# Products of zeros on TensorE from the first microsecond, and the first stages by head pairs, in a fused attention and FFN kernel

## The chip, the cores and the metric

One core of one Trainium2 chip. Times are device microseconds of one execution; a quoted time is the median of the runs named. The span is the time from a kernel's first to its last instruction in the trace. In the views of the profile PE stands for TensorE's products, PEld for its weight loads, DVE for VectorE, ACT for ScalarE and POOL for GpSimd. PSUM is the memory of the kernel's `ps_` tiles, which products are written to; a bank is the place of one such tile. A load *lands* when its data are all there.

## The reference, cut to what matters

```python
# q, k, v: (8, 8, 1024, 64)   batch, heads, tokens, head size;   E, F: (64, 1024)
k_proj = einsum('ks,bhsd->bhkd', E, k)
v_proj = einsum('ks,bhsd->bhkd', F, v)
scores = q @ k_proj^T / 8
attn = exp(scores) / sum(exp(scores))
x = (attn @ v_proj), heads side by side: (8192, 512)
h = maximum(x @ w_in, 0)          # w_in: (512, 2048)
out = (h * h) @ w_out             # w_out: (2048, 512), out float32
```

## The kernel before

Eight batches. While the FFN of one batch runs, pieces of the attention of the next stand between its groups of matmuls. Only batch 0 has no FFN to hide behind, so it has a routine of its own, `first_stages`, that works on half of the tokens first so that the FFN can start early. All matmuls take bf16. The order of instructions on every engine is the order in which they are written, and the trace has them in it: K's first half landed at 8.72 us, and its products started at 9.11, behind two fillers written ahead of them that started at 8.14.

The loads of batch 0 are issued from the GpSimd queue in the order of need, one behind the other:

```python
for s in (slice(0, 4), slice(4, 8)):
    load_heads(K_first, k, s)            # K in two halves (heads 0-3, 4-7)
...
load_q_half(0, slice(0, H))              # Q, first half of the tokens
for s in (slice(0, 4), slice(4, 6), slice(6, 8)):
    load_heads(V_first, v, s)            # V in three pieces
nc.scalar.preload_act_table_set("natural_log_exp_and_others")
ones = const_pool.tile([P, 32], BF16, name="ones")
nc.vector.memset(ones[:], 1.0)
...                                      # then w_in in pieces, w_out, Q's second half
```

The first stages. `filler` multiplies data that are there anyway, into a PSUM bank that nobody reads, to keep TensorE active:

```python
def first_stages(self):
    def filler(n):
        ps = ffn_psum("ps_fill")
        for _ in range(n):
            nc.tensor.matmul(ps[:], lhsT=ET[:, 0:2, :], rhs=ET[:], start=True, stop=True)
    filler(2)
    self.project_k(0)                    # 8 products 128x256, waits for K's first half
    filler(1)
    self.transpose_k(0)
    self.project_k(1)                    # waits for K's second half
    filler(2)
    self.transpose_k(1)
    filler(1)
    for g in range(2):
        self.half_transpose_q(0, g, ffn_psum)      # waits for Q
    for g in range(2):
        self.half_scores(0, g)
        self.half_exponentials(g)
    heads = [slice(0, 4), slice(4, 6), slice(6, 8)]
    self.project_v(heads[0])
    self.copy_v(heads[0])
    self.half_sums(0, apart=True)
    self.half_sums(1)
    self.half_reciprocals(0)
    self.half_reciprocals(1)
    self.half_values(0)
    for s in heads[1:]:
        self.project_v(s)
        self.copy_v(s)
    self.half_values(1)
    for g in range(2):
        for e in range(2):
            self.half_normalize(0, g, e)
```

Then the FFN. Its opening takes four groups at once, column block by column block (16 products), which is why "the fifth group" is a landmark below.

The softmax here doesn't subtract the row's maximum and nothing guards it: scores larger than these inputs give would overflow.

Of the kernel before, what the change touches and what calls it, by code (L numbers as in the profile page):

```python
# [8 lines left out]
P = 128  # L9
F32 = mybir.dt.float32  # L10
BF16 = mybir.dt.bfloat16
# [9 lines left out]
def kernel(  # L21
# [11 lines left out]
    nc = tc.nc  # L33
# [20 lines left out]
    const_pool = ctx.enter_context(tc.tile_pool(name="const", bufs=1))  # L54
# [15 lines left out]
    def att_psum(shape, dtype):  # L70
        return aps.tile(shape, dtype, tag="att", name="ps_att")

    def ffn_psum(name, shape=(P, 512), dtype=F32):
        return fps.tile(list(shape), dtype, tag="ffn", name=name)
# [4 lines left out]
    def load(name, src, b):  # L79
        t = qkv_pool.tile([P, H, NI * D], BF16, name=name)  # L80
        nc.gpsimd.dma_start(t[:], rows(src, b))  # L81
        return t
# [18 lines left out]
    ident = const_pool.tile([P, P], BF16, name="ident")  # L101
# [3 lines left out]
        load_heads(V_first, v, s)  # L105
    nc.scalar.preload_act_table_set("natural_log_exp_and_others")
    ones = const_pool.tile([P, 32], BF16, name="ones")
    nc.vector.memset(ones[:], 1.0)


# [22 lines left out]

    LO, HI = slice(0, 64), slice(64, 128)
    ET, FT = (const_pool.tile([P, NI, KP], BF16, name=n) for n in ("ET", "FT"))

    def E_and_F():
        for t, src, copy in ((ET, e_f32[0], nc.vector.tensor_copy), (FT, e_f32[1], nc.scalar.copy)):
            e_bf = soft_pool.tile([KP, S], BF16, tag="expT", name="e_bf")
            copy(e_bf[:], src[:])  # L140
            ps = ffn_psum("ps_E", (P, NI, KP), BF16)
            view = e_bf[:].rearrange("k (p i) -> k i p", i=NI)
            for i in range(NI):
                nc.tensor.transpose(ps[:, i, :], view[:, i, :], ident[0:KP, 0:KP])
            copy(t[:], ps[:])
# [7 lines left out]
    def combine_weights(q4, name):  # L153
        js = slice(4 * q4, 4 * q4 + 4)
        o, a, b = {"T1": (T1, W12, W11), "T2": (T2, W22, T1), "T3": (T3, W22, W12), "T4": (T4, W21, T2)}[name]
        nc.vector.tensor_tensor(out=o[:, js], in0=a[:, js], in1=b[:, js], op=ALU.subtract)
# [4 lines left out]
    class Attention:  # L161
# [127 lines left out]
                self.vp[:, s].rearrange("k h e d -> k e h d"),  # L289
                self.ps["vp", s.start][:].rearrange("k (h d e) -> k e h d", d=D // 2, e=2))  # L290

        def half_transpose_q(self, c, g, psum):
            ps = psum("ps_q", (P, 4, 2, P), BF16)
            for h in range(4):
                for n in range(2):
                    nc.tensor.transpose(
                        ps[:, h, n], self.Q[:, 4 * g + h, (2 * c + n) * P:(2 * c + n + 1) * P], ident[:])
            qt = self.qT[:].rearrange("p (h n) t -> p h n t", n=NT)
            nc.vector.tensor_copy(qt[:, 4 * g:4 * g + 4, 2 * c:2 * c + 2], ps[:])

        def half_scores(self, c, g):
            ps = self.ps["s", g] = att_psum([P, 2, 2, TH], F32)
# [52 lines left out]
            )  # L355

        def first_stages(self):
            def filler(n):
                ps = ffn_psum("ps_fill")
                for _ in range(n):  # L360
                    nc.tensor.matmul(ps[:], lhsT=ET[:, 0:2, :], rhs=ET[:], start=True, stop=True)

            filler(2)
            self.project_k(0)
            filler(1)
            self.transpose_k(0)
            self.project_k(1)
            filler(2)
            self.transpose_k(1)
            filler(1)  # L370
            for g in range(2):
                self.half_transpose_q(0, g, ffn_psum)
            for g in range(2):
                self.half_scores(0, g)
                self.half_exponentials(g)
            heads = [slice(0, 4), slice(4, 6), slice(6, 8)]
            self.project_v(heads[0])
            self.copy_v(heads[0])
            self.half_sums(0, apart=True)
            self.half_sums(1)  # L380
            self.half_reciprocals(0)
            self.half_reciprocals(1)
            self.half_values(0)
            for s in heads[1:]:
                self.project_v(s)
                self.copy_v(s)
            self.half_values(1)
            for g in range(2):
                for e in range(2):
                    self.half_normalize(0, g, e)  # L390

        def second_half(self, stage, g):
            if stage == 0:
                self.half_transpose_q(1, g, lambda name, shape, dtype: att_psum(shape, dtype))
            elif stage == 1:
                self.half_scores(1, g)
                self.half_exponentials(g)
            elif stage == 2:
                self.half_sums(g)
                self.half_values(g)  # L400
                self.half_reciprocals(g)
            else:
                for e in range(2):
                    self.half_normalize(1, g, e)
# [27 lines left out]
        53: "values 1 0, values 1 1", 54: "normalize 1 0", 55: "normalize 1 1",  # L432
    }
    SECOND_HALF = {
        7: "second_half 0 0", 9: "second_half 1 0", 10: "second_half 0 1",
        11: "second_half 2 0", 12: "second_half 1 1", 13: "second_half 3 0",
        15: "second_half 2 1", 16: "second_half 3 1",
    }
# [12 lines left out]
    def calls(table, n):  # L451
        for c in filter(None, table.get(n, "").split(", ")):
            name, *args = c.split()
            yield name, [int(a) for a in args]
# [232 lines left out]
    with tc.manual_schedule(engines=ORDERED):  # L687
        def load_batch(b):

            if b < B:  # L690
                order = [("K_sb", k), ("V_sb", v), ("Q_sb", q)] if b == 1 else [("Q_sb", q), ("K_sb", k), ("V_sb", v)]
                t = {n: load(n, src, b) for n, src in order}
                return Attention(b, t["Q_sb"], t["K_sb"], t["V_sb"])

        E_and_F()
        cur = Attention(0, Q_first, K_first, V_first)
        cur.first_stages()
        nxt = ahead = None
        for b in range(B):
            for n, g in enumerate(ffn_groups(b, cur.xT)):  # L700
                if b == 0:
                    for name, args in calls(SECOND_HALF, n):
                        getattr(cur, name)(*args)
                    for name, args in calls(WEIGHTS, n):
                        combine_weights(args[0], name)
                    if n == 31:
                        nxt = load_batch(1)
                if nxt:
                    for name, args in calls((BATCH_1, BATCH_2, PIECES)[min(b, 2)], n):
                        getattr(nxt, name)(*args)  # L710
                    if n == (35, 14, 1)[min(b, 2)]:
                        ahead = load_batch(b + 2)
                    if b and n == 33 and ahead:
                        ahead.transpose_q()
                    if b and n == 53 and ahead:
                        ahead.project()
                g()
            if b == 0:
                nxt.normalize(1, 1)
            cur, nxt, ahead = nxt, ahead, None  # L720
# [30 lines left out]
```

## Time and profile before

| what | kernel before | where from |
|---|---|---|
| device time | 483.68 us (483.64 to 484.29) | median of 3 runs |
| span of the profiled execution | 482.4 us | profile page |
| device time less span | 1.76 us (1.71 to 1.83) | mean of 48 runs, made beside the experiments and as `k1` |
| TensorE products | 3630, busy 470.3 us | profile page |
| VectorE instructions | 382 | profile page |
| loads of batch 0: K's first half, Q's first half | landed at 8.72 and 14.24 us | issue plus time to landing |

TensorE is busy 97% of the span, so there are some 12 us to be had at the very most, and 8.4 of them lie before 21 us. How the stages are read is told in the prediction.

### The profile page before, as it was taken

Reading aid. Unit: us, or ns where it says so; the run is one execution under the profiler, and the core shown is the slowest. Engines: PE = TensorE matmul, PEld = TensorE weight load, DVE = VectorE, ACT = ScalarE, POOL = GpSimd, SP = SyncE. Lnnn points to the kernel's source line nnn. Section 1 sums busy time; section 2 is a strip of 40 time slices with the busy share of each in tenths; the row PEclk is TensorE's granted clock in tenths of the full one; section 3 lists DMA queues with packets and bytes.
Section 4 is the critical chain, followed back from the end, with each engine's and each line's share of the span. In section 5 each row is a group of like instructions: output and inputs, shape, how many; then the busy total and the mean of one; then the engine's idle time right before and its main releaser. Section 6 shows DMA issues by size and latency. Waiting matters only on the chain.

```text
span 482.4 us, 8423 instructions
## 1 busy us (share of the span) xinstructions
PE 470.3 (97%) x3630; PEld 292.6 (61%) x3630; DVE 314.1 (65%) x382; ACT 261.5 (54%) x413; POOL 34.7 (7%) x48
## 2 busy tenths in 40 slices
PE   4899999999999999999999999999999999999997
PEld 2544676475574746657475665747557474666656
DVE  1478955554958559493776848667494855948383
ACT  2387544758427564466635667176662756545351
POOL 6540020020020001000010000100000000000000
PEclk9999999999999999999999999999999999999999
DMA  9999989579989086941859147690702102020202
GB/s 155 203 204 207 168 181 200 137 120 229 180 128 229 12 175 88 180 94 50 153 86 227 22 115 131 91 200 1 165 11 75 25 1 88 1 88 0 88 1 87
DMA packets 72789, 55.46 MB, mean 115 GB/s; under 512 B 33968, under 2 KB 64944, under 8 KB 72752
## 3 DMA queue, kind: packets, MB, share of 16 engines
q0 software_dynamic: 30624, 29.36, 39.4%
q1 hardware_dynamic: 42128, 25.56, 21.1%
q8 instruction: 28, 0.46, 0.4%
q14 instruction: 9, 0.07, 0.0%
HBM read 59.24 MB, written 16.78 MB: 158 GB/s over the span
## 4 chain that ended last, share of the span: by engine, by line
PE 92%; DVE 3%; DMA 3%; ACT 1%; POOL 1%; issue 0%; POOLq 0%
PE ps_h L459 44%; PE ps_y L479 23%; PE ps_z L479 11%; PE ps_x L479 6%; DMA V_sb<-in_v_dram 3%; PE ps_kv L180 2%; PE ps_att L221 2%; PE ps_att L206 2%; DVE hsq L521 1%; DVE s L473 1%; PE ps_v L284 0%; DVE xT L246 0%; DVE xT L351 0%; PE ps_kv L181 0%; ACT h_relu L513 0%; POOL K_sb L93 0%
## 5 line engine op out<-in xcount | busy, mean ns | idle before, releaser
L459 PE MATMUL ps_h<-xT,w_in 128*128 128x512 bf16 x1024 | 224.8, 379 | 0.2 <-DVE xT L351 0.2
L521 DVE TENSOR_TENSOR hsq<-h_relu 128x1024 bf16<-128x1024 f32 x123 | 149.9, 1222 | 75.0 <-ACT h_relu L513 74.2
L513 ACT ACTIVATE h_relu<-ps_h 128x512 f32<-128x512 f32 x255 | 149.4, 597 | 63.4 <-PE ps_h L459 63.0
L459 PEld LDWEIGHTS <-w_in 128*128 128x128 bf16 x1024 | 99.7, 98 | 117.7 <-issue 1.9
L479 PEld LDWEIGHTS <-s 128*128 128x128 bf16 x1024 | 98.5, 98 | 19.8 <-issue 8.7
L479 PEld LDWEIGHTS <-hsq 128*128 128x128 bf16 x768 | 73.8, 98 | 17.3 <-issue 3.8
L479 PE MATMUL ps_y<-T,s 128*128 128x256 bf16 x512 | 62.4, 273 | 0.0
L246 DVE TENSOR_TENSOR xT<-ps_att,rs 128x1024 bf16<-128x1024 f32 x28 | 33.4, 1215 | 17.6 <-ACT rs L236 17.0
L473 DVE TENSOR_TENSOR s<-hsq 128x1024 bf16<-128x1024 bf16 x64 | 43.5, 683 | 0.0
L591 ACT COPY o_sb<-ps_y 128x512 f32<-128x512 f32 x15 | 8.8, 586 | 53.8 <-PE ps_y L479 53.7
L213 ACT ACTIVATE expT<-ps_att 128x1024 bf16<-128x1024 f32 x28 | 27.2, 1025 | 14.0 <-PE ps_att L206 14.0
L479 PE MATMUL ps_x<-w_out,hsq 128*128 128x256 bf16 x256 | 33.2, 273 | 0.0
L479 PE MATMUL ps_y<-w_out,hsq 128*128 128x256 bf16 x256 | 33.2, 273 | 0.0
L595 DVE TENSOR_TENSOR o_sb<-ps_z,p_b 128x512 f32<-128x512 f32 x16 | 11.0, 688 | 33.8 <-issue 19.9
L479 PE MATMUL ps_y<-T,hsq 128*128 128x256 bf16 x256 | 30.9, 272 | 0.0
L479 PE MATMUL ps_z<-T,s 128*128 128x256 bf16 x256 | 30.6, 273 | 0.0
L479 PE MATMUL ps_z<-w_out,s 128*128 128x256 bf16 x256 | 30.6, 273 | 0.0
L591 ACT COPY p_b<-ps_y 128x512 f32<-128x512 f32 (+1 forms) x17 | 9.4, 556 | 25.9 <-PE ps_y L479 25.8
L81 POOL DMA_DIRECT2D Q_sb<-in_q_dram x7 | 6.1, 876 | 227.7 <-DMA qT<-Q_sb 227.2
L473 DVE TENSOR_TENSOR s<-s,hsq 128x1024 bf16<-128x1024 bf16 x32 | 21.8, 684 | 0.3
L473 DVE TENSOR_TENSOR s<-hsq,s 128x1024 bf16<-128x1024 bf16 x32 | 21.7, 682 | 0.0
L591 ACT COPY p_a<-ps_y 128x512 f32<-128x512 f32 (+1 forms) x17 | 9.4, 561 | 21.8 <-PE ps_y L479 21.6
(75 smaller groups left out, 233.0 us busy)
## 6 DMA issues: line engine op xcount, KB each, us to landing
out_dram<-o_sb SPq DMA_DIRECT2D x30, 512.0 KB, 3.8
K_sb<-in_k_dram POOLq DMA_DIRECT2D x7, 1024.0 KB, 15.3
V_sb<-in_v_dram POOLq DMA_DIRECT2D x7, 1024.0 KB, 22.4
Q_sb<-in_q_dram POOLq DMA_DIRECT2D x7, 1024.0 KB, 9.4
w_out<-in_moe_w_out_dram POOLq DMA_DIRECT2D x4, 512.0 KB, 13.2
w_in<-in_moe_w_in_dram POOLq DMA_DIRECT2D x7, 256.0 KB, 10.0
K_sb<-in_k_dram POOLq DMA_DIRECT2D x2, 512.0 KB, 8.5
out_dram<-o_sb SPq DMA_DIRECT2D x3, 256.0 KB, 2.1
```

The source lines that it names most:

```text
L180: nc.tensor.matmul(ps[0:KP, :], lhsT=ET[:, i, :], rhs=kv[:, :, i, :], start=f, stop=l)
L206: nc.tensor.matmul(ps[o, bank, :], lhsT=self.kT[r, 2 * pr + j, :], start=True, stop=True, rhs=self.qT[r, NT * (2 * pr + j):NT * (2 * pr + ...
L213: nc.scalar.activation(e[:], self.ps["s", pr][:], AF.Exp, scale=SCALE)
L221: nc.tensor.matmul(ps[32 * j:32 * j + 32, a, :], lhsT=weights(o, 4 * g + j), rhs=self.exp[2 * g + j // 2][o, bank, :], start=True, stop=Tr ...
L246: nc.vector.tensor_tensor(out=self.xT[:, 2 * g + e].rearrange("p a n t -> p a (n t)"), in0=self.ps["v", g, e][:], in1=self.rs[g][:], op=AL ...
L459: nc.tensor.matmul(ps[:], lhsT=w_in_blk(cb, fb), rhs=xT[:, cb, :, 2 * ch:2 * ch + 2], start=(cb == 0), stop=(cb == NCB - 1),)
L473: nc.vector.tensor_tensor(out=s[o][:, js], in0=x, in1=y, op=op)
L479: nc.tensor.matmul(ps[tb] if len(ps) == 2 else ps[0][:, tb], lhsT=lhs[:, j, tb * P:(tb + 1) * P], rhs=rhs[:, j], start=first and n == 0 an ...
L513: nc.scalar.activation(r[:, n], ps[:], AF.Relu)
L521: multiply = lambda: nc.vector.tensor_tensor(out=o, in0=r[:], in1=r[:], op=ALU.mult)
L591: nc.scalar.copy(to[:, t], ps)
L595: nc.vector.tensor_tensor(out=to[:, t], in0=ps, in1=more[:, t], op=ALU.add)
```

## The change

Its intent: in the trace of the kernel before, the first eight K products (from 9.11 us) take 1.92 us and the second eight (from 12.00) 1.06, and the clock's first record of full speed is at 11.23. So let TensorE multiply zeros from the first microsecond until E and then K land; let the copies of Q go in head pairs over two engines; and put the sums and normalizations of the first stages in an order that lets the FFN start earlier, with group 1's values inside the FFN's opening.

```diff
+    zeros = const_pool.tile([P, 512], BF16, name="zeros")
+    nc.vector.memset(zeros[:], 0.0)
     nc.vector.memset(ones[:], 1.0)
...
+    def filler(n):
+        ps = ffn_psum("ps_fill")
+        for _ in range(n):
+            nc.tensor.matmul(ps[:], lhsT=zeros[:, 0:P], rhs=zeros[:], start=True, stop=True)
...
         def first_stages(self):
-            filler(2)
+            filler(3)
             self.project_k(0)
-            filler(1)
+            filler(3)
             self.transpose_k(0)
             self.project_k(1)
-            filler(2)
+            filler(3)
             self.transpose_k(1)
-            filler(1)
-            for g in range(2):
-                self.half_transpose_q(0, g, ffn_psum)
+            for n in range(4):
+                self.half_transpose_q(
+                    0, range(2 * n, 2 * n + 2), ffn_psum, nc.scalar.copy if n == 1 else nc.vector.tensor_copy)
...
+            self.half_sums(0, apart=True)
             self.project_v(heads[0])
             self.copy_v(heads[0])
-            self.half_sums(0, apart=True)
             self.half_sums(1)
             self.half_reciprocals(0)
             self.half_reciprocals(1)
             self.half_values(0)
+            self.half_normalize(0, 0, 0)
             for s in heads[1:]:
                 self.project_v(s)
                 self.copy_v(s)
+            self.half_normalize(0, 0, 1)
+
+        def last_of_first(self):
             self.half_values(1)
-            for g in range(2):
-                for e in range(2):
-                    self.half_normalize(0, g, e)
+            for e in range(2):
+                self.half_normalize(0, 1, e)
...
     SECOND_HALF = {
-        7: "second_half 0 0", ...
+        1: "last_of_first", 7: "second_half 0 0", ...
...
+        filler(10)
         E_and_F()
```

## The prediction

> **What bounds the kernel now.** I began with the page's busy row and chain. TensorE is busy 470.3 of 482.4 us and carries 92% of the chain that ended last; the one DMA in that chain is V of the first batch. So there are two questions: how much of the 12 us without TensorE work lies in the stages that the change touches, and whether what is won there reaches the end. The stretches (columns: busy us and count of each engine, granted clock, DMA share, GB/s) answer the first:
>
> ```profile
> 0.00:8.72 8.72, 1.93 (x18) 1.29 (x18) 1.20 (x3) 2.80 (x3) 6.91 (x14) 1.00 0.79 139
> 8.72:14.24 5.52, 4.97 (x30) 2.69 (x28) 1.65 (x6) 0.11 (x1) 1.40 (x2) 1.00 1.34 201
> 14.24:21.05 6.81, 5.76 (x129) 3.81 (x129) 3.14 (x8) 4.34 (x7) 3.54 (x5) 1.00 1.28 204
> 21.05:24.70 3.65, 3.61 (x16) 1.56 (x16) 2.17 (x4) 0.64 (x2) 2.21 (x4) 1.00 1.30 200
> 24.70:53.30 28.60, 28.51 (x201) 13.11 (x201) 24.10 (x30) 23.30 (x39) 4.86 (x6) 1.00 1.25 206
> ```
>
> TensorE idles 6.8 us before K's first half, 0.55 and 1.05 us in the next two stretches, and practically never after 21 us. But the last column is level at 200 to 206 GB/s from 8.7 to 53.3 us: one uninterrupted stream of loads, the slower of two racers. So I read each early load's landing (issue plus time to landing): K 8.7 and 11.6 us; Q's first half 14.2; V 16.8, 18.1 and 19.4; w_in's first pieces 20.0, 20.7, 22.05, 23.3 and 24.55; Q's second half 25.9 and 29.8; w_in 27.2, 28.5, 31.1.
>
> Then I looked for the last place where TensorE meets the stream. It is the projection of batch 1, in the 34th group of the first FFN (columns: start, us, engine, line, operation):
>
> ```profile
> 53.03 0.40 PE L180 MATMUL ps_kv<-K_sb,ET 128*64 128x512 bf16 x1
> 53.32 0.38 PE L181 MATMUL ps_kv<-V_sb,FT 128*64 128x512 bf16 x1
> 53.32 0.40 PE L180 MATMUL ps_kv<-K_sb,ET 128*64 128x512 bf16 x1
> 53.53 0.38 PE L181 MATMUL ps_kv<-V_sb,FT 128*64 128x512 bf16 x1
> ...
> 54.82 0.38 PE L181 MATMUL ps_kv<-V_sb,FT 128*64 128x512 bf16 x1
> ```
>
> and the same stage of batch 2, where the data had landed earlier:
>
> ```profile
> 92.79 0.40 PE L180 MATMUL ps_kv<-K_sb,ET 128*64 128x512 bf16 x1
> 92.79 0.40 PE L181 MATMUL ps_kv<-V_sb,FT 128*64 128x512 bf16 x1
> ...
> 93.03 0.38 PE L180 MATMUL ps_kv<-K_sb,ET 128*64 128x512 bf16 x1
> ```
>
> In batch 2 V's first product starts with K's, at 92.79, and the next pair 0.24 us later. In batch 1 K's starts at 53.03 and V's only at 53.32. V was issued at 30.31 and takes 23.0 us to land:
>
> ```profile
> V_sb<-in_v_dram POOLq DMA_DIRECT2D x1, 1024.0 KB, 23.0
> ```
>
> that is 53.3 us. So **TensorE already waits about 0.29 us there for a transfer that the change does not touch.** "Idle" does not show it, because a pipelined K product's modelled end covers the gap.
>
> [...] the first eight K products (128x256) take 1.92 us, or (1.92 - 0.42) / 7 = 0.214 us apiece; the second eight, from 12.00 on, take 1.06 us, or 0.11. [...] V's issue occupies POOL for 0.88 us of the 23.0 to landing. Hence landings, not POOL's busy time, decide here.
>
> **The change part by part.**
>
> (1) Zero products. 13 more 128x512 fillers (10 in front, and 3+3+3 in place of 2+1+2+1). Ten at half speed cost about 0.40 us apiece (the two at 8.14 start 0.40 apart), about 4 us, from about 1.2 to at most 5.6. E's transposes, ready at 4.98, slip by up to 0.6 us, but TensorE then waits for F's cast until 7.49 anyway. Three warm fillers behind F (0.22 each, from the spacing of the 128x512 FFN products) end near 8.8, K's first half having landed at 8.7. The first K products now run warm and save 0.10 x 8 = 0.8 us, and nobody pays for the later fillers, since the next K half lands at 11.6. The second K half can start at 11.65 in place of 12.00. All of this ends at one line: Q's first half lands at 14.24, and before the change its transposes already start at 14.29. **Warmth buys 0 us past that point.**
>
> (2) Q by head pairs. The copies that gate group 0's scores were one of 0.68 us after 8 transposes (15.69 scores). Now: four transposes end at 14.67, DVE copies the pair by 15.1; pair 1's transposes end at 14.9 and ACT (0.59 us for 128x512 bf16, as FT's copy) is done by 15.5; scores complete about 15.6. The first exponential starts near 15.9 in place of 16.15, the second near 16.85 in place of 17.07: -0.2 us.
>
> (3) Sums ahead of V's projection. TensorE waits for the first exponential (about 16.95) and only then projects V, which landed at 16.78: projection from 17.1, not 16.82, and its copy at 18.6, not 18.35. So the values of group 0 come about 0.25 us later, while the reciprocals come 0.3 us earlier (19.16 for 19.48).
>
> (4) Normalization of group 0 between V's copies, group 1's values after the first FFN column block. Values 0 end at about 19.05, first normalization 19.2 to 19.9, V's two remaining projections end at 19.6 and 20.3 (before: 19.4 and 20.1). The first FFN products need w_in (20.0, 20.7) and start about 20.35 in place of 21.05. Then group 1's values (0.41 plus changeovers) stand inside the opening, and its 16 products take 3.6 us: 20.35 + 3.6 + about 0.5 = 24.4. Group 4 needs the PSUM bank of group 0, whose ReLU follows the first product of the last column block: about 24.4 in place of 24.70. **Gain at this point: 0.3 us.**
>
> (5) The 28.6 us that follow are the same instructions. The landings leave room for 0.3: the tightest, w_in at 28.49, is used at 29.03. So batch 1's projection is reached near 52.75, and V still lands at 53.3. The wait grows from 0.29 to about 0.6 us.
>
> Sum: -0.3 at 24.4, +0.3 at 53.3, **0 after that**; the rest is the old program at TensorE's pace.
>
> **The rivals.** (a) The gain survives: if V of batch 1 landed earlier, 0.3 us, perhaps 0.5, would reach the end, 483.2. For it: TensorE is busy without break from 21 us. Against: V is behind everything in one queue, and each issue on POOL from 9 us to 29 us follows a landing, so nothing that TensorE does earlier starts a transfer earlier. (b) The new order costs more than I count: in (3) TensorE stands in front of a projection whose data are there, and V's slot or DVE's order may cost 0.3 to 0.5 us more. The start of FFN would be 0.2 later than before; but the 0.29 us of waiting at 53.3 would swallow this too: 483.7 to 483.9. (c) The zero fill on DVE or longer POOL issues delay the start of the stream by 0.1 to 0.2 us: 483.8. (d) Warm clock as the whole intent: 0.8 us faster K projection, plus warm fillers, would give 482.7 if K's path set the end. Against it stands Q's landing at 14.24.
>
> **Range and chances.** The centre is the old 483.68 less a little for (a): 483.6. The old kernel's own three runs span 0.65 us, so the range is mostly that and the rivals: 483.0 to 484.2. 2% is 9.7 us; all of TensorE's idle time before 21 us is 8.4, so faster by that is out, and nothing in the change adds 9.7: 0.005, 0.99, 0.005.
>
> **What would show it.** Right: fillers from near 1.2 us; first K products about 0.11 us apart; Q's transposes still at about 14.3; first exponential about 15.9; first FFN product about 20.4; fifth group about 24.4; K's first product of batch 1 near 52.75 and V's first at 53.3 still, the gap between them doubled. Wrong: V of batch 1 landing clearly earlier or later than 53.3 (then the end moves with it); the first FFN product after 21; a new TensorE wait after 55 us.

(Two passages that no trace of this case shows are cut where marked. No term of the sum is among them: -0.3 us at the fifth group and +0.3 at the wait for V leave 0, and the centre is 483.6. That ten zero products in front are enough for the first K products to take 0.11 us apiece and not 0.214, as (1) has it, was my estimate.)

## More of the kernel before

In the 34th group stands the projection of batch 1's K and V, with the products of the two taking turns:

```python
BATCH_1 = {
    33: "project", 34: "copy_kp, transpose_q, copy_vp", 37: "copy_v_down",
    ...
```

## The result, and the profile after

| | before | after |
|---|---|---|
| device time, 6 runs each, alternating on one chip | 483.81 us (483.52 to 484.58) | 484.15 us (483.97 to 485.81) |
| ratio after / before, 95% interval | | 1.0009 (0.9994 to 1.0025): the same |
| span of the profiled execution | 482.4 us | 482.1 us |
| device time less span, mean | 1.76 us | 2.15 us |

A ratio here and below is the mean time of one kernel's runs over that of the other's of the same rounds, so it is not quite the ratio of the medians beside it. The 2.15 is the mean of all 11 runs of the changed kernel (2.09 to 2.19); the 1.76 is that of 48 runs of the kernel before (1.71 to 1.83), made beside the experiments and as `k1`.

The time is unchanged as a class, and 0.34 us higher in the median where I had expected 0.1 less. The profiled span shows nothing of a loss: it is 0.3 us *shorter*. To find what happened I read the same stretches as before; columns are from:to, length, then busy us and count of PE, PEld, DVE, ACT and POOL, granted clock, DMA share and GB/s. After:

```profile
0.00:8.72 8.72, 6.96 (x29) 2.78 (x29) 1.79 (x4) 2.91 (x3) 7.29 (x15) 1.00 0.87 154
8.72:14.24 5.52, 5.42 (x38) 3.18 (x38) 1.94 (x6) 0.00 (x0) 1.47 (x3) 1.00 1.34 201
14.24:21.05 6.81, 5.28 (x112) 3.35 (x109) 3.38 (x8) 4.82 (x8) 2.93 (x4) 1.00 1.28 203
21.05:24.70 3.65, 3.61 (x31) 1.39 (x30) 1.80 (x3) 0.72 (x2) 2.40 (x4) 1.00 1.32 201
...
53.30:482.40 429.10, 425.18 (x3240) 269.70 (x3234) 281.86 (x335) 230.19 (x363) 15.74 (x18) 1.00 0.54 105
```

and the long rest in the kernel before:

```profile
53.30:482.40 429.10, 425.51 (x3240) 270.09 (x3238) 281.86 (x335) 230.29 (x363) 15.77 (x18) 1.00 0.54 105
```

After 53.3 us the two are one program: 3240 products each, and the same busy time within 0.4 us. From the last V product of batch 1's projection to the end it is 427.54 to 427.58 us in every trace with the projection at its old place but `k7` (428.32; it waits 0.78 us for a later V at 133 us). So everything that differs between these two spans differs before 55 us. TensorE is now busy 6.96 us of the first 8.72, as was meant. (The clock column says 1.00 in these early stretches only because no record of the clock precedes the first letting-up. The durations of the products tell the clock there.)

**The start.** TensorE before (start, us, engine, line, operation):

```profile
9.11 1.92 PE L262 MATMUL ps_k<-K_sb,ET 128*64 128x256 bf16 x8
...
12.00 1.06 PE L262 MATMUL ps_k<-K_sb,ET 128*64 128x256 bf16 x8
14.29 0.40 PE L296 MATMUL ps_q<-ident,Q_sb 128*128 128x128 bf16 x4
```

and after:

```profile
1.20 4.45 PE L143 MATMUL ps_fill<-zeros 128*128 128x512 bf16 x10 [1.20 <-DVE ones L110]
...
7.49 1.46 PE L143 MATMUL ps_fill<-zeros 128*128 128x512 bf16 x3
8.89 1.85 PE L270 MATMUL ps_k<-K_sb,ET 128*64 128x256 bf16 x8
...
13.84 0.95 PE L304 MATMUL ps_q<-ident,Q_sb 128*128 128x128 bf16 x14
```

The fill starts at 1.20 as expected, but the K products still take 1.85 us for eight, the half-clock figure (1.88 in `k2` below, where the recorded clock is 0.50; 1.06 for the second eight here, behind the letting-up). The clock's first record of full speed is at 10.54 us (11.23 before). K's first half had landed at 7.80 in this run. The three fillers behind F, still at half clock (1.46 us; the next three, from 10.66 on, took 0.82), held TensorE until 8.89. So here the fillers *delayed* K by 1.09 us (before, K started 0.39 us behind its landing, after two fillers). The delay passes down: Q had landed at 13.14, its transposes start at 13.84. Before, they started 0.05 us behind the landing.

**The FFN's opening.** Before, one uninterrupted row, then after:

```profile
21.05 4.03 PE L459 MATMUL ps_h<-xT,w_in 128*128 128x512 bf16 x17 [0.19 <-DVE xT L351]
```

```profile
19.74 0.60 PE L467 MATMUL ps_h<-xT,w_in 128*128 128x512 bf16 x2
20.86 0.60 PE L467 MATMUL ps_h<-xT,w_in 128*128 128x512 bf16 x2 [0.52 <-DMA w_in<-in_moe_w_in_dram]
21.40 0.41 PE L328 MATMUL ps_att<-expT,vp 64*32 64x256 bf16 x16
21.75 3.25 PE L467 MATMUL ps_h<-xT,w_in 128*128 128x512 bf16 x13
```

The FFN opens 1.31 us earlier, and the fifth group comes at 24.62 in place of 24.70, only 0.08 earlier. Between them stands a wait of 0.52 us for a piece of w_in. The chain that ended last names the same transfer: where the kernel before had V of batch 0 in it, this one has w_in.

```profile
PE ps_h L467 44%; PE ps_y L487 23%; PE ps_z L487 11%; PE ps_x L487 6%; DMA w_in<-in_moe_w_in_dram 3%; PE ps_kv L188 3%; PE ps_att L229 2%; PE ps_att L214 2%; DVE hsq L529 1%; DVE s L481 1%; DVE xT L254 0%; POOL V_sb L93 0%; ACT h_relu L521 0%; POOL K_sb L93 0%; DVE xT L359 0%
```

That piece (128 KB) was issued at 7.05 us and took 13.8 us to land, so it landed at 20.82, 1.89 us behind the piece ahead of it (18.93). Pieces of this size otherwise land 0.64 us apart (these two 0.68 before). What else used the DMA engines in that time? The rows of the queues between 18.7 and 19.8 us of the changed kernel (packets, MB, share of 16 engines):

```profile
q0 software_dynamic: 276, 0.21, 125.0%
q8 instruction: 1, 0.02, 5.4%
```

One packet of kind "instruction". 5.4% of 16 engines over 1.1 us is 0.95 us of one engine; the trace's record of it says 16384 bytes from 18.77 us on. I read it as TensorE's next block of program: the page of either kernel has 28 packets in this queue, all of 16384 bytes, and from one to the next TensorE runs 250 of its 7260 instructions (3630 products and as many weight loads) in the mean before and 251 after; `k9` below moves it with the number of TensorE's instructions. It is not free here: the packet near this place took 0.89 to 0.98 us of one DMA engine in the 18 traces (0.89 before, 0.95 after). The trace's semaphore records time a landing in 16 steps, which I read as the shares of the 16 DMA engines. Of the piece ahead, the 16 steps came from 18.33 to 18.93 us. Of the late piece 15 had come by 19.57, and the last came at 20.82. So, by this reading, one share of sixteen was held up, and the piece that shares an engine with the packet lands late (1.25 us behind its other 15 steps). Before, the same packet came at 20.55 us, and no piece was late.

**Batch 1's projection.** After:

```profile
52.95 0.40 PE L188 MATMUL ps_kv<-K_sb,ET 128*64 128x512 bf16 x1
52.95 0.40 PE L189 MATMUL ps_kv<-V_sb,FT 128*64 128x512 bf16 x1
```

V's first product now starts with K's. V had landed at 52.59 in this run, against 53.27 before, so the wait of 0.29 us is gone.

**One account of the span.** The fifth group and the projection of batch 1 are 28.32 us apart in every trace with the old placement of the projection (28.45 in one). So the span is fixed by four terms: when Q lands, how long after it the transposes start, the time from there to the fifth group, and the wait for V. For the two profiled executions:

| term, us | before | after | difference |
|---|---|---|---|
| Q's first half lands | 14.24 | 13.14 | -1.10 |
| Q's transposes start after it by | 0.05 | 0.70 | +0.65 |
| from there to the fifth group | 10.42 | 10.78 | +0.36 |
| to the projection of batch 1 | 28.32 | 28.32 | 0 |
| wait for V there | 0.29 | 0 | -0.29 |
| sum | | | -0.38 (span: 482.38 to 482.06, -0.32) |

The split of these terms is that of two traces and does not repeat. In `k1`, the kernel before once more, the transposes start 0.58 us behind Q's landing, and the fifth group comes 10.01 us later. Their sum repeats better: from Q's landing to the fifth group it is 10.46 before and 10.59 in `k1`, 11.48 after and 11.37 in `k2`, the changed kernel once more.

The first line is not the work of the change: over nine traces with the old order of the first stages Q lands at 13.16 to 15.23 us (median 13.61), and over nine with the new order at 13.11 to 14.88 (median 13.35). Without it the changed program has *lost* a microsecond to its own data and got it back from loads that happened to land early. (Q's first of 16 steps came at 12.84 before and 12.55 after, its last at 14.24 and 13.14: most of the 1.10 us is one trace's slowest shares.) The experiments take the other terms apart.

### The profile page after: what moved, and what is told of

Its sections match the earlier page's. It is cut to its first block, busy times and chain, and to the rows that moved or that the text cites. A ratio compares the mean times of both kernels' runs of the same rounds, so it can differ in the third digit from the quotient of the medians. Undisturbed runs are those within 1.5% of the kernel's fastest.

```text
span 482.1 us, 8454 instructions
## 1 busy us (share of the span) xinstructions
PE 475.0 (99%) x3643; PEld 293.6 (61%) x3643; DVE 314.9 (65%) x384; ACT 261.9 (54%) x414; POOL 34.4 (7%) x48
## 4 chain that ended last, share of the span: by engine, by line
PE 92%; DMA 3%; DVE 3%; POOL 1%; ACT 1%; issue 0%; POOLq 0%
PE ps_h L467 44%; PE ps_y L487 23%; PE ps_z L487 11%; PE ps_x L487 6%; DMA w_in<-in_moe_w_in_dram 3%; PE ps_kv L188 3%; PE ps_att L229 2%; PE ps_att L214 2%; DVE hsq L529 1%; DVE s L481 1%; DVE xT L254 0%; POOL V_sb L93 0%; ACT h_relu L521 0%; POOL K_sb L93 0%; DVE xT L359 0%
## 5 line engine op out<-in xcount | busy, mean ns | idle before, releaser
L487 PEld LDWEIGHTS <-s 128*128 128x128 bf16 x1024 | 98.5, 98 | 19.8 <-issue 8.7
L599 ACT COPY o_sb<-ps_y 128x512 f32<-128x512 f32 x15 | 8.8, 586 | 53.8 <-PE ps_y L487 53.7
L603 DVE TENSOR_TENSOR o_sb<-ps_z,p_b 128x512 f32<-128x512 f32 x16 | 11.0, 688 | 33.5 <-issue 19.8
```

The source lines that it names most:

```text
L487: nc.tensor.matmul(ps[tb] if len(ps) == 2 else ps[0][:, tb], lhsT=lhs[:, j, tb * P:(tb + 1) * P], rhs=rhs[:, j], start=first and n == 0 an ...
L599: nc.scalar.copy(to[:, t], ps)
L603: nc.vector.tensor_tensor(out=to[:, t], in0=ps, in1=more[:, t], op=ALU.add)
```

## The experiments

"Clock" in this section is a run's mean granted TensorE clock; one stretch of 6.83 us at half speed within 483.7 us makes it 0.993. Half speed before the first letting-up is not in it.

### The two kernels again

No edit: the kernel before as `k1`, the changed one as `k2`.

> The kernel before, unchanged, to see what repeats. Theory 'phase': the early loads differ from run to run by up to 1 us (K's first half landed at 8.72 in one trace of before and 7.80 in the one of after) and have nothing to do with the change; then this trace may show K's first half anywhere from 7.8 to 8.8, V of batch 1 anywhere from 52.5 to 53.4, and the wait for V at 53.0 is 0 or 0.3 us accordingly. Theory 'change': the zero products or the order move the loads; then this trace again shows 8.7 and 53.3 and the 0.29 us wait. Ratio to before 1.000 within 0.001 either way; device time less span 1.75 us as in the first trace if that is a property of the kernel, up to 2.1 if not.

> The changed kernel, unchanged. 'Phase': its K half and V landings fall anywhere in the same ranges as those of before, and the ratio is 1.000 within 0.001. 'Change': K at 7.8 and V of batch 1 at 52.6 again. The clock is let up near 10.5 again if the zero products do not count for it or are too sparse[...]. First FFN product 19.7, fifth group 24.6, projection of batch 1 at 52.95, each within 0.3.

`k1`: 483.76 us (6 runs), ratio 1.0002 (0.9986 to 1.0017). `k2`: 484.69 us (5 runs, 484.37 to 485.81), ratio 1.0020 (1.0007 to 1.0034). The small loss is real on this chip: 0.76 us in the median, about 0.4 of it in the span (482.5 for 482.1). Device time less span was 1.75 for `k1` and 2.17 for `k2`, so this difference repeats in every single run.

`k2`'s profile caught one of its worst runs (485.81 us):

```profile
4.26:7.67 3.41, 2.02 (x20) 1.29 (x18) 1.46 (x2) 1.04 (x1) 3.41 (x6) 1.00 1.02 148
7.67:14.50 6.83, 6.18 (x26) 3.02 (x25) 0.93 (x3) 0.59 (x1) 1.53 (x3) 0.50 1.31 199
```

The fill brought the clock up at 4.26 us, and 3.41 us later it was taken away again until 14.50, although TensorE was busy 2.02 us of that first stretch (the transposes of E and F, between which it waits for F's cast). The K products that the fill was meant to speed up then ran at half clock (1.88 us for eight), and half-speed fillers stood between them:

```profile
9.81 1.88 PE L270 MATMUL ps_k<-K_sb,ET 128*64 128x256 bf16 x8 [0.65 <-DMA K_sb<-in_k_dram]
...
13.34 1.61 PE L270 MATMUL ps_k<-K_sb,ET 128*64 128x256 bf16 x8
16.16 0.51 PE L304 MATMUL ps_q<-ident,Q_sb 128*128 128x128 bf16 x6
```

K's second half had landed at 12.22 and Q at 14.88; their products start 1.12 and 1.28 us later. The mean clock is under 0.998 in 5 of the changed kernel's 11 runs and in none of the 48 runs of the kernel before. (That kernel has another bad case: 8 of its 48 runs are over 485 us with a clock of 0.999 or 1.000. No profile caught one. A late first letting-up, which this mean does not count, is a candidate; it is not shown.)

### The fill alone, and the order alone

`k3` is the kernel before with the zeros, the 10 fillers in front and the 3+3+3 in the path, and the old order of everything else. `k4` is the changed kernel without these:

```diff
# k3, against the kernel before
+    zeros = const_pool.tile([P, 512], BF16, name="zeros")
+    nc.vector.memset(zeros[:], 0.0)
-            filler(2) ... filler(1) ... filler(2) ... filler(1)     # products of ET
+            filler(3) ... filler(3) ... filler(3)                   # products of zeros
+        filler(10)
# k4, against the changed kernel: the same lines the other way round
```

> Before plus the zero products alone (10 in front, 3, 3, 3), old order of the first stages. My theory: Q's transposes wait for Q's landing, so the fill is worth 0: fifth group at 24.7 within 0.2, ratio 1.000 within 0.001. Rival: the fill is the useful part and lets the clock up by 6 us, K's chain ends 0.8 us sooner: ratio 0.999 or less, fifth group at 24.2 or sooner.

> Before plus the new order and the head pairs alone, old fillers (2, 1, 2, 1 of E's transpose). My theory: first exponential 0.2 us sooner behind Q's transposes, first FFN product 0.7 us sooner, but the loads of w_in and V stop it: fifth group at 24.4 to 24.7, ratio 1.000 within 0.001. Rival: the order is the useful part and carries its 0.3 us to the end: ratio 0.9994.

| | device time | ratio to before | device time less span | span, median | runs with clock under 0.998 |
|---|---|---|---|---|---|
| before, same chip | 483.93 | | 1.78 | 482.1 | 0 of 11 |
| `k3` fill alone | 484.26 | 1.0013 (0.9999 to 1.0026) | 1.99 | 482.25 | 4 of 6 |
| `k4` order alone | 484.32 | 1.0005 (0.9993 to 1.0017) | 2.14 | 482.2 | 0 of 5 |

The clock's coming and going belongs to the fill. `k3`'s profile caught a good run, in which the fill starts at 1.19 and the clock was let up at 6.45 us and stayed:

```profile
8.23 1.06 PE L270 MATMUL ps_k<-K_sb,ET 128*64 128x256 bf16 x8
...
10.72 1.06 PE L270 MATMUL ps_k<-K_sb,ET 128*64 128x256 bf16 x8 [0.38 <-DMA K_sb<-in_k_dram]
...
13.37 1.07 PE L304 MATMUL ps_q<-ident,Q_sb 128*128 128x128 bf16 x16 [0.53 <-DMA Q_sb<-in_q_dram]
```

Here K's products take 1.06 us in place of 1.9, as I had predicted, and against the trace of the kernel before they are worth nothing, also as predicted: TensorE waits 0.38 us for K's second half and 0.53 us for Q, which landed at 13.32. From there to the fifth group it is 10.48 us, before it was 10.46. (The fifth group came at 23.81 and not near 24.7, as I expected, because Q landed 0.92 us sooner.)

But that trace of the kernel before was a good one. In the eight traces with the old order and without the zeros the clock first came up at 10.85 to 15.36 us, and Q's transposes started 0.05 to 1.81 us behind Q's landing. In the three with the latest clock (`k16` 12.86, `k14` 13.58, `k11` 15.36) the fifth group stands 11.52, 11.00 and 11.91 us behind Q's landing, in the other five 10.46 to 10.59. So a fill that keeps its clock, as in this trace of `k3`, wins nothing in most executions and by this estimate (against 10.48) 0.5 to 1.4 us in some, and at its worst it loses over a microsecond. In device time the two do not add up to a gain.

The order's own worth can be read in traces whose data were all in time. Times are us after Q's first transpose:

| trace | first exponential | values of group 0 | first FFN product | fifth group | opening (difference of the last two) |
|---|---|---|---|---|---|
| old order: `k1`, `k12`, `k14`, `k16` (data in time) | 1.85 | 3.95 | 6.36 | 10.01 | 3.65 |
| old order: before (V just in time) | 1.86 | 4.12 | 6.77 | 10.42 | 3.65 |
| new order: `k2`, `k4`, `k6` (data in time) | 1.64 | 4.54 | 5.90 | 10.09 | 4.19 |
| new order: after | 1.64 | 4.54 | 5.90 | 10.78 | 4.88 |

(Each cell is the same within 0.02 for all traces of its row.) The new order opens the FFN 0.46 us earlier and pays 0.54 in the opening, where group 1's values now stand. With all data there it is worth 0.08 us *less* than nothing. It is worth something only against a stream that keeps V back: the kernel before lost 0.41 us to V in this stretch (10.42 for 10.01), and the new order, which wants V 0.6 us later (first V product 2.95 us after the transposes, for 2.33), does not. 10.42 less 10.09 is the 0.3 us that the prediction counted. But the changed kernel then lost 0.69 us (10.78 for 10.09) to the late piece of w_in. (`k5` and `k8` below have the same piece late and lose 0.80 and 1.28: 10.89 and 11.37.)

### The fill's operands and its amount

```diff
# k5, against the changed kernel
-    nc.vector.memset(zeros[:], 0.0)
+    nc.vector.memset(zeros[:], 1.0)
# k6                                   # k7
-            filler(3)   (three times)   -            filler(3)   (three times)
+            filler(6)                   # the ten in front stay
# k8: F's cast and transposes go behind K's first half
-        E_and_F()        -> E_or_F(0)
-            filler(3)    -> filler(6)
             self.project_k(0)
-            filler(3)    -> E_or_F(1)
```

In the expectations of `k5` and `k8`, 'windows' names a guess of mine from six traces: that the share of products other than transposes in stretches of 3.41 us (the length of the stretch in `k2` from 4.26 to 7.67) decides about the clock. Its rule is cut from `k5` where marked, since the later traces did not bear it out.

> The changed kernel with the fill tile set to 1.0 in place of 0.0. Theory 'windows': [...] ones change nothing: about half of the runs show a mean clock of 0.993 to 0.996, the median is 484.2 to 484.7. Rival 'zeros do not count': with ones the clock is up by 4.5 to 8 us in each run and stays, no run under 0.999, no run over 485.

> The changed kernel with 6, 6, 6 zero products between the steps of the K path in place of 3, 3, 3. Theory 'fill in the path': in-order TensorE runs them ahead of K's work, 0.43 us apiece while the clock is half; with the clock up the 9 more cost up to 0.65 us per place where K waits for nothing else. So the first Q transposes come 1 to 2.5 us later than Q's landing and the span grows by 1 to 2 us: 485 to 486.5. Rival 'more fill keeps the clock up, K waits for its loads anyway': same as the changed kernel or better, no run under 0.999.

> The changed kernel with its 10 zero products in front and none between the steps of the K path. 'Fill in the path': K's products start when K lands, even at half clock; Q's transposes within 0.3 us of Q's landing or of K's own chain; but the stretch from 6 to 10 us is emptier, so the clock comes up late, 13 to 17 us, in most runs: span 481.8 to 483. Rival 'clock decides all': without the fill each run is like the slow ones, 483.5 and more.

> The changed kernel with F's transposes moved from before K's first projection to behind it, and 6 zero products in their place, so that from 1.2 us to K's landing no stretch of 3.41 us has more than 0.8 us of transposes or idling. 'Windows': the clock is up by 8.0 us in each run and stays (mean 0.998 or more), K's first products run 0.11 us apart, Q's transposes start within 0.1 us of Q's landing, no run over 485, span 481.4 to 482.2; the device time stays 2.1 above the span, so 483.6 to 484.3. Rival 'phase of the loads alone': slow runs of 485.8 as often as in the changed kernel.

| | device time | ratio to before | span, median | runs with clock under 0.998 |
|---|---|---|---|---|
| before, same chip | 484.33 | | 482.6 | 0 of 11 |
| `k5` ones for zeros | 484.34 | 0.9997 (0.9979 to 1.0016) | 482.15 | 1 of 4 |
| `k6` 6+6+6 in the path | 485.25 | 1.0018 (0.9996 to 1.0041) | 483.1 | 2 of 4 |
| `k7` none in the path | 486.66 | 1.0042 (1.0012 to 1.0071) | 484.55 | 2 of 4 |
| `k8` F behind K | 484.93 | 1.0009 (0.9990 to 1.0029) | 482.8 | 3 of 6 |

Ones do as zeros do, as far as four runs tell. Twice the fill in the path costs about 1 us of span (483.1 against `k5`'s 482.15); no fill in the path costs more, against my expectation of 481.8 to 483: in `k7`'s profile the clock comes up only at 16.94, the first exponential moves from 1.64 to 2.51 us behind Q's transposes, and two runs have mean clocks of 0.986 and 0.982 (487.81 and 488.01 us). Of that profile's span of 483.4, 0.75 us is the later wait for V named above and not the start. So three fillers at each place are better than none and than six, and what they buy is that the start is not worse than before.

`k8` was my attempt to keep the clock from being taken back, by a rule that I had drawn from the earlier traces: no stretch of 3.41 us with more than 0.8 us of transposes or idling before K lands. It failed. Three of its six runs still have clocks of 0.993 to 0.996. Its profile shows TensorE busy 2.33 us of a stretch of 3.41 in which the clock stayed, and `k6`'s shows it busy 2.34 us of one after which the clock was taken. Busy time alone does not decide it. Without the transposes (the products with the identity) the stretch of `k8` has 1.76 us and the two that cost the clock 1.05 (`k6`) and 0.76 (`k2`), so a rule that leaves transposes out would fit these three. But in `k7` the clock came up at 16.94 after a stretch with 0.89 such, while in `k11` a stretch with 2.87 (from 8.53 us on) did not let it up. By what rule the clock is let up and taken back stays open.

### Where the program fetch falls

`k9` moves TensorE's block boundary and little else of weight: four of the ten fillers in front become 24 products of one column.

```diff
+    def small_filler(n):
+        ps = ffn_psum("ps_fill")
+        for _ in range(n):
+            nc.tensor.matmul(ps[:, 0:1], lhsT=zeros[:, 0:P], rhs=zeros[:, 0:1], start=True, stop=True)
-        filler(10)
+        filler(6)
+        small_filler(24)
```

> The changed kernel with 6 zero products of 512 columns and 24 of one column in front in place of 10 of 512: about the same time, but 36 more TensorE instructions. In each trace so far TensorE's program is fetched in one packet of 16384 bytes near here (18.8 in the changed kernel, 20.55 before), it occupies one DMA engine for 0.9 to 0.97 us, and in 8 of 10 traces the load that lands next, or next but one, comes 0.6 to 1.4 us late; in the changed kernel that is w_in's second piece, for which TensorE waits 0.5 us. Theory 'program fetch': the fetch moves up to 17.5 to 18.4, the late piece is V's last or w_in's first, w_in's second piece lands 0.6 to 0.7 after the first, TensorE does not wait for it, and the fifth group comes at 24.1 to 24.5. Rival 'stream of loads, fixed place': the second piece is late again whatever the program.

The packet came at 17.47 us in place of 18.77. The piece that was then in the stream was the last of V: it landed 2.45 us behind the one ahead of it, in place of 1.41 in the changed kernel; 15 of its 16 steps had come by 18.47 us, the last came at 19.57. And w_in's second piece kept its pace, 0.67 us behind the first (the last step of each is 0.8 to 0.9 us behind its other 15):

```profile
20.18 1.09 PE L472 MATMUL ps_h<-xT,w_in 128*128 128x512 bf16 x4
21.21 0.41 PE L333 MATMUL ps_att<-expT,vp 64*32 64x256 bf16 x16
21.55 3.68 PE L472 MATMUL ps_h<-xT,w_in 128*128 128x512 bf16 x15
```

The wait of 0.52 inside the opening is gone. The fifth group came at 24.43, which is 10.46 us behind Q's transposes; V's late piece cost 0.31 of the 0.37 above 10.09. Across the traces the late piece follows the fetch: the earlier TensorE's block is fetched, the earlier in the stream is the piece that lands late (neighbouring rows overlap by up to 0.2 us).

| trace | fetch at, us | late piece |
|---|---|---|
| `k15`, `k9` | 17.16, 17.47 | V's last |
| after, `k8`, `k5` | 18.77, 19.06, 19.08 | w_in's second |
| `k3`, `k10`, `k1`, `k13`, `k6`, `k14` | 18.88, 19.51, 19.86, 19.88, 20.13, 20.52 | w_in's third |
| `k16`, `k11`, `k4`, `k7` | 20.42, 20.77, 21.14, 21.43 | w_in's fourth |
| before, `k2`, `k12` | 20.55, 21.23, 21.32 | none |

In 15 of the 18 traces one load lands late, by 0.6 to 1.4 us. In each of the 15 the last of the late piece's 16 steps comes 0.5 to 1.4 us behind the other 15; in the piece ahead of it that is 0.2 us at most. That the fetch decides which piece is late is shown by `k9`, whose other loads kept their pace. The three traces that escape are those in which the 16 steps of a piece were already 1.4 (before), 1.7 (`k2`) and 2.2 us (`k12`) apart before the fetch, for 0.4 to 1.2 us in the other 15: there a share that loses 0.9 us can still come before the last one. In device time `k9` is 483.96 us, ratio 0.9998 (0.9978 to 1.0018), and its span has the median 481.8 (before, on that chip: 482.0). Since every microsecond of this stretch is full of needed loads (200 to 204 GB/s from 8.72 to 24.70 us in both kernels), the fetch can be moved from one to another, and the gain is a few tenths.

### The wait for V of batch 1

`k10` is the kernel before with batch 1's projection one group later, so that V has time to land.

```diff
-        33: "project", 34: "copy_kp, transpose_q, copy_vp", 37: "copy_v_down",
+        34: "project", 35: "copy_kp, transpose_q, copy_vp", 37: "copy_v_down",
```

> The kernel before with the projection of batch 1 and what hangs on it one FFN group later. Theory 'V is the floor': K's and V's first products now start together, as in batch 2, and the 0.1 to 0.3 us of waiting are gone: span shorter by that, ratio 0.9995. Rival 'the floor is elsewhere': same span, the wait shows up somewhere else.

483.81 us, ratio 0.9998 (0.9975 to 1.0020). V's first product starts 0.01 us behind K's. At the old place the projection would have stood at 52.12 in this run (fifth group at 23.80, plus 28.32), and V landed at 52.40, so a wait of 0.28 us is lifted. Another took its place a little later:

```profile
56.75 0.93 PE L479 MATMUL ps_z<-T,s 128*128 128x256 bf16 x7
57.92 0.92 PE L479 MATMUL ps_y<-T,s 128*128 128x256 bf16 x7 [0.24 <-ACT p_a L591]
```

Seven products at 0.11 us from 56.75 end their turn at 57.52; the next starts at 57.92, 0.40 us later, because the bank that it writes must first be copied out by ScalarE (`p_a`, 57.28 to 57.87), which does the two copies of projected V before it. In the kernel before this copy ends at 58.14 and the bank is next written at 58.64, so nobody waits. The gain of about 0.3 went into that, and a little more: from the fifth group to the end `k10` takes 457.85 us, the kernel before 457.68.

### Device time outside the span

The changed kernel has two VectorE instructions more on the page (384 for 382), and one more if the sequencer's rows of that engine are counted. Four kernels ask whether that is what the 0.39 us outside the span go with. Each is the kernel before with one small edit near the start, on an engine that has nothing to do there:

```diff
# k11: one more on VectorE
+    spare = const_pool.tile([P, 32], BF16, name="spare")
+    nc.vector.memset(spare[:], 0.0)
# k12: one more on ScalarE
+    nc.scalar.copy(spare[:], ones[:])
# k13: one less on VectorE
-    nc.vector.memset(ones[:], 1.0)
+    nc.gpsimd.memset(ones[:], 1.0)
# k14: three more on VectorE
+    for t in spare:                  # three tiles
+        nc.vector.memset(t[:], 0.0)
```

> Device time less span is 1.72 to 1.83 in all 28 runs of before, 1.94 to 2.02 in the fill alone, 2.08 to 2.22 in each kernel with the new order. One more VectorE instruction (a memset that nobody reads) in before: 1.98 if the number of VectorE's instructions makes it, 1.76 if not.

> One more ScalarE instruction (a copy that nobody reads) in before: device time less span 2.1 if the number of ScalarE's instructions makes it, 1.76 if not.

> The kernel before with its one VectorE memset moved to GpSimd: one VectorE instruction fewer. If the number of VectorE's instructions sets the time outside the span, that time falls under 1.76, to about 1.55; if 1.76 is its floor, it stays at 1.76. Span as before (481.6 to 483), perhaps 0.1 more because GpSimd issues w_in later.

> The kernel before with three VectorE memsets that nobody reads. VectorE count: device time less span 2.14, as in the changed kernel, which also has three VectorE instructions and copies more. Otherwise 1.76 or 1.99. Span as before.

| VectorE rows, with the sequencer's, against before | kernels | device time less span, mean us |
|---|---|---|
| -1 | `k13`, `k16` | 1.79, 1.75 |
| 0 | before (48 runs, with those of `k1`), `k10` | 1.76, 1.78 |
| 0, one more on ScalarE | `k12` (one run) | 1.8 |
| +1 | `k3`, `k11` (one run) | 1.99, 1.99 |
| +2 | `k4`, `k15` | 2.14, 2.09 |
| +3 | after, `k14` | 2.15, 2.16 |
| +3 | `k5` to `k9` | 2.11 to 2.17 |

`k14` touches nothing that the change touches and has the whole of the 0.4 us. ScalarE's instruction has no such effect in its one run. Taking one away wins nothing, so the kernel before already stands at a floor. That the part outside the span goes with the number of VectorE instructions is shown, for these five counts. Where it lies, the trace shows too: behind the last instruction. The records of the clock run on past it and end 2.01 to 2.04 us behind it in the six traces at 0 or -1, 2.23 in the two at +1, 2.35 and 2.36 in the two at +2, and 2.37 to 2.40 in the eight at +3; and the device time of each of the 18 profiled runs is 0.24 to 0.25 us less than the time from the first instruction to the end of these records. There are semaphore updates there but no instructions of the program, so what is done in that time, and why VectorE's count lengthens it, is not shown.

In device time `k13` is 483.79 us, ratio 0.9989 (0.9974 to 1.0004), and `k14` 484.72, ratio 1.0004 (0.9987 to 1.0021), on a chip where the kernel before took 484.69 (11 runs). Over a few runs the spans vary by more than the effect; the difference from the span, run by run, does not.

### The parts that looked good, together

`k15` is `k9` with the projection one group later and the ones set by GpSimd; `k16` is `k10` with the ones set by GpSimd.

> The changed kernel with the fetch moved up (6 zero products of 512 columns and 24 of one), batch 1's projection one group later and the ones set on GpSimd. If the early gain reaches the end once these three are out of its way: span 481.3 to 481.9, outside 1.9 to 2.1, so 483.3 to 483.9, ratio 0.999. If not: span 482.1 as before, 484.1.

> The kernel before with batch 1's projection one group later and the ones set on GpSimd, without fill and new order. Span 481.6 to 482.2, outside 1.55 to 1.76: 483.3 to 483.8, ratio 0.999. If k15 is no better than this, fill and order are worth nothing even with their obstacles away.

`k15`: 484.67 us, ratio 1.0004 (0.9991 to 1.0016), span 482.6 in the median (before, same chip: 482.9), 2.09 outside. `k16`: 484.25 us, ratio 0.9998 (0.9985 to 1.0012), span 482.5, 1.75 outside. Neither beats the kernel before beyond the interval, and no version does.

## Why the prediction was right or wrong

The class held, and 484.15 lies just inside the upper end of the range, 484.2. The number did not hold: 484.15 for 483.6, and on the wrong side of the kernel before.

**The step that failed is the one that turns the span into a time: "The centre is the old 483.68 less a little".** Every term in the sum was a term of the span, and the span did about what the sum says (medians of 482.1 before and 482.2 after). That is luck: the terms themselves came out otherwise, as the steps below show, and cancelled. The device time rose all the same, because the part outside the span rose from 1.76 to 2.15 us with the VectorE instructions that the change adds. This +0.39, behind the last instruction, was in no step and in no rival, and it is all of the measured +0.34. (In `k2`, on its chip, it is about half of 0.76; the rest is span.) The 0.55 us between prediction and result are this 0.34, the gain of 0.08 that I had hoped for, and 0.13 by which the kernel before was itself slower in the later runs (483.81 for 483.68).

**Step (1), zero products, failed in its middle and held in part at its end.** "The first K products now run warm" is not what the profiled run did: the clock came up at 10.54, fillers at 0.43 us apiece held K back by 1.09 us, and Q's transposes started 0.70 us behind their landing, where I had them wait for it. I had put the fillers at 0.22 us, which takes for granted that ten in front are enough. Sometimes they are: 5 of 11 runs have a mean clock that says that it came up and was taken back. The moment varies: with ten fillers in front the clock first came up at 4.26 us in `k2`, 6.45 in `k3` and 10.54 in the changed kernel's first trace. My step had one moment in it, by which the clock would be up before K, and that was an estimate which no trace had shown. The last sentence of the step, that warmth buys 0 us past Q's landing, held for the trace that I had: `k3` shows TensorE waiting for K and for Q (0.38 and 0.53 us) with its clock at full speed since 6.45. As a rule it fails, because I took one trace's clock and one trace's landing of Q for constants: in the kernels without the zeros whose clock came late, at 12.86 us and after, Q's transposes started 0.99 to 1.81 us behind Q's landing.

**Steps (2) and (3)** held in their mechanism. The first exponential came 1.64 us behind Q's transposes in place of 1.86 (predicted: 0.2 less). The values of group 0 came 0.42 us later by the same measure (4.54 for 4.12), somewhat more than the 0.25 predicted.

**Step (4), "Gain at this point: 0.3 us", had the right mechanism and lacked a term.** (Its sum, 20.35 + 3.6 + 0.5, is 24.45 and not 24.4, which makes the gain 0.25.) Undisturbed, the new order is 10.09 us where the kernel before took 10.42: 0.33. The missing term is TensorE's own program. With 13 products more, and their weight loads, the same block of instructions is reached earlier; its fetch moved from 20.55 to 18.77 us, into the flight of the piece of w_in that the FFN's opening needs, and cost 0.69 us. `k9` shows it by moving the fetch: the wait of 0.52 us inside the opening is gone, and another piece is late. Rival (c) came nearest to this, in asking what the change does to the stream of loads, but it looked at issues alone.

**Step (5), "The wait grows from 0.29 to about 0.6 us", did not show itself.** The projection was reached at 52.95, not at 52.75, and V had landed at 52.59. The floor is real but moves: V lands between 52.3 and 53.7 us in these traces, and the wait is there in before (0.29), `k1` (0.13), `k3` (0.34) and `k13` (0.20) and absent in most others. I took one trace's landing for a constant. As `k10` shows, lifting it brings the next wait.

**The rivals.** (b), that the new order costs more than counted, is what the data-in-time traces show (10.09 for 10.01), though by 0.08 and not by 0.3 to 0.5 us. (d), warm K products as a gain, is out by `k3` against the trace of the kernel before, and is open for executions in which the clock comes late. (a) would need what step (4) and the stream did not give.

## What to carry to other kernels

A change of a fraction of a per cent has to be compared in device time and in span separately, since the first can rise by 0.4 us while the second falls. Here feeding TensorE early bought nothing past the landing of the data that it then waited for (`k3`: K's products in 1.06 us and not 1.92, then 0.53 us of waiting for Q), and the fed products must be short enough at *half* clock not to stand in front of those data (in the changed kernel three of 1.46 us together held K back by 1.09). Where loads follow one another without a gap, count the instructions of the busiest engine: here its program came through the same DMA engines (a packet took 0.89 to 0.98 us of one), and adding instructions moved the moment at which one of the loads was late (the packet from 20.55 to 18.77 us with 13 products more, to 17.47 in `k9`).
